# Powers by scans, a mask from eight one-hot products, decay on TensorE, and a new order for the first units of a fused attention and feed-forward kernel

## The chip, the cores and the metric

The kernel runs on one core of a Trainium2 chip. The metric is the device time of one execution in microseconds; the kernel before takes 632.63 us as the median of 3 runs (631.36 to 633.64). The profiled execution is a run of its own.

## The reference

Two stages follow each other: a linear attention with a decay `lam` for each head, worked in blocks along the sequence, and a feed-forward network with a squared ReLU. Sizes: batch 4, 8 heads, 768 positions, head size 64, `x` of 3072 x 512, hidden size 2048.

```
Dmask = where(rel >= 0, lam ** rel, 0)            # rel = i - j inside a block
lam_pow = lam ** (pos + 1); lam_block = lam ** block
for each block b:
    intra = (qb @ kb.T * Dmask) @ vb
    inter = (qb * lam_pow) @ kv_state
    out[b] = intra + inter
    kv_state = lam_block * kv_state + (kb * lam ** (block - 1 - pos)).T @ vb
x = out as (tokens, heads * head size)
h = relu(x @ w_in); result = (h * h) @ w_out
```

## The kernel before, in words

**Tiling.** The attention is cut into 24 tiles `t` of 128 positions, six of them to a batch element (`NCB`); each holds all 8 heads as 4 pairs (`NPR`), so that two heads of 64 rows fill 128 partitions. The feed-forward part takes four attention tiles at a time (a group `m` of 512 tokens, six groups). For each group it goes through 16 slices `f` of the hidden size. `hidden(m, f)` (L397) is 12 matmuls of 128 x 512, and `project(m, f)` (L420) is another 12. Both keep single-precision accuracy by splitting each operand into a high part and a low remainder (`xh` and `xl`, `wh` and `wl`, `gh` and `gl`) and adding three products; `square` (L408, three operations of ScalarE) and `rest` (L415, one of VectorE) make `gh` and `gl` from `h`.

**Weights.** They are loaded as 64-bit numbers (`raw`) in 17 units `u` (`wload`, L106). Only two buffers of `raw` and two of `A` exist. The conversion of a unit is `first_hi` and `first_lo` (ScalarE, L119 and L125), `clamp`, `shift`, `sign`, `rounded` (VectorE, L133 to L150), then `upper` (ScalarE, to `wh`) and `lower` (VectorE, to `wl`). `hidden(0, f)` needs unit `f` whole, its first four matmuls only `wh`. All of that happens once, in group 0; groups 1 to 5 find the weights in place.

**Attention.** For a tile, `scores` (L298) makes the products of keys and queries, `masked` (L318, two VectorE operations) multiplies them with `mask`, `prep_q` and `prep_k` (L308 and L312, GpSimd) scale queries and keys, `news` (L331) makes the new part of the state, `within` (L339) and `before` (L347) the two parts of the output, `update` (L354) the new state `kv`, and `split` (L365) writes `xh` (ScalarE) and returns a function for `xl` (VectorE). The old state's decayed copy `kvd` comes from `decay` (L386, two GpSimd operations), and `update` adds it on VectorE.

**Order.** The order on every engine is the order in which the code is written; nothing is scheduled by a tool. Four attention tiles (0 to 3) must be ready before `hidden(0, 0)`; their order, with units 0 to 2 of the weights in between, is written out by hand from L456 to L529. Tiles 4 to 7 follow inside group 0: `scores` at step 0 of four slices, `masked` at step 1, `attend` at step 2, `decay` at step 3. `turn` (L167) is a tiny GpSimd copy that reads `wl`, so that the GpSimd work written behind it starts only after a certain `lower`. All loads are issued by SyncE in the order of the code.

**Prologue.** The powers of `lam` are worked out on 8 partitions (L212 to L237): repeated squares, a correction of their rounding, six dependent steps on one column (L226) and seven doublings of the row `pz` (L234). Three matmul stages then spread them: `get_near` (8 products with 8 columns), `get_wide` (3 products that shift `near` by partitions), and copies of `wide` into `mask`; `get_qpow` makes `qpow` from one product of 512 columns. `warm(n)` issues matmuls on a zeroed tile.

## Time and profile before

| what | value |
| --- | --- |
| median of 3 runs | 632.63 us |
| profiled execution, its own time | 632.65 us |
| its span in the trace | 630.7 us |
| granted TensorE clock, mean of the span | 0.991 |
| TensorE busy | 620.7 us (98%) |
| VectorE busy | 222.6 us (35%) |
| ScalarE busy | 233.8 us (37%) |
| GpSimd busy | 87.9 us (14%) |

How to read what follows. Times in the trace are microseconds from the start of the span; 1.95 us lie between the span and the execution's time. In a row of the timeline the first column is the start, the second the duration, then come the engine, the line of the code, the operation and what it writes and reads; `x16` is the number of merged instructions (a single-precision matmul leaves two records), and brackets give the idle time before it and what ended it. Instructions of an engine overlap a little at their ends, so the step from one start to the next is the better cost. PE is TensorE, PEld its weight loads, DVE VectorE, ACT ScalarE, POOL GpSimd and SP SyncE; SPq is SyncE's queue that issues loads. PEclk is the granted clock of TensorE, 1.00 for full speed. "GB/s" and "DMA share" tell what the loads moved.

### The profile page before, as it was taken

How to read it: one execution, taken by the hardware profiler on the slowest of the kernel's cores; microseconds unless marked ns; L12 is line 12 of the kernel's file. 1: busy time of each engine (PE TensorE's matmuls, PEld its weight loads, DVE VectorE, ACT ScalarE, POOL GpSimd, SP SyncE). 2: the span in 40 equal slices, each digit the busy share in tenths (PEclk: the TensorE clock that was granted, in tenths of full speed). 3: DMA queues.
4: the chain of work that ended last, by engine and by line, in shares of the span. 5: the costliest groups of instructions: out<-in, count | busy, mean ns of one | idle time of the engine just before them, and what ended most of it. 6: DMA issues, size and time to landing. Idle time of an engine off the chain costs nothing.

```text
span 630.7 us, 8978 instructions
## 1 busy us (share of the span) xinstructions
PE 620.7 (98%) x3744; PEld 509.8 (81%) x3744; DVE 222.6 (35%) x341; ACT 233.8 (37%) x383; POOL 87.9 (14%) x106
## 2 busy tenths in 40 slices
...
GB/s 313 285 161 210 183 221 236 73 124 67 2 68 6 62 68 100 34 68 2 68 8 126 68 1 100 34 1 68 73 61 68 1 2 0 68 1 1 0 1 67
DMA packets 18488, 48.81 MB, mean 77 GB/s; under 512 B 2064, under 2 KB 2064, under 8 KB 18448
## 3 DMA queue, kind: packets, MB, share of 16 engines
...
## 4 chain that ended last, share of the span: by engine, by line
PE 95%; DVE 2%; DMA 1%; issue 1%; POOL 0%; ACT 0%; POOLq 0%; SPq 0%; DVEq 0%
PE h L402 41%; PE acc L429 14%; PE acc L430 14%; PE acc L434 14%; PE att L303 3%; PE h L342 2%; PE h L349 2%; PE h L334 1%; PE att L342 1%; PE att L65 1%; DMA qk_sb<-in_kT 1%; DMA raw<-in_w 1%; PE att L349 1%; PE acc L303 0%; PE att L334 0%
## 5 line engine op out<-in xcount | busy, mean ns | idle before, releaser
L417 DVE TENSOR_TENSOR gl<-h,gh 128x512 fp32r<-128x512 f32 x96 | 66.3, 691 | 351.7 <-ACT h L412 351.7
L409 ACT ACTIVATE h<-h 128x512 f32<-128x512 f32 x96 | 55.9, 582 | 308.1 <-PE h L402 308.1
L429 PE MATMUL acc<-wh,gh 128*128 128x512 f32 x384 | 150.0, 391 | 0.0
L430 PE MATMUL acc<-wl,gh 128*128 128x512 f32 x384 | 149.4, 389 | 0.0
L434 PE MATMUL acc<-wh,gl 128*128 128x512 f32 x384 | 149.0, 389 | 0.0
L402 PE MATMUL h<-xh,wh 128*128 128x512 f32 x384 | 105.4, 396 | 0.7 <-ACT xh L369 0.7
L402 PE MATMUL h<-xh,wl 128*128 128x512 f32 x384 | 103.0, 390 | 0.2 <-DVE wl L161 0.2
L402 PE MATMUL h<-xl,wh 128*128 128x512 f32 x384 | 102.7, 389 | 0.0
L429 PEld LDWEIGHTS acc<-wh,gh 128*128 128x128 f32 x384 | 72.2, 188 | 15.7 <-issue 0.5
L402 PEld LDWEIGHTS h<-xh,wl 128*128 128x128 f32 x384 | 72.0, 188 | 15.9 <-DVE wl L161 0.6
L402 PEld LDWEIGHTS h<-xl,wh 128*128 128x128 f32 x384 | 72.1, 188 | 15.1
L430 PEld LDWEIGHTS acc<-wl,gh 128*128 128x128 f32 x384 | 72.2, 188 | 14.8
L434 PEld LDWEIGHTS acc<-wh,gl 128*128 128x128 f32 x384 | 72.1, 188 | 15.0
L402 PEld LDWEIGHTS h<-xh,wh 128*128 128x128 f32 x384 | 70.4, 188 | 17.0 <-ACT xh L369 0.9
L411 ACT ACTIVATE gh<-h 128x512 fp32r<-128x512 f32 x96 | 57.6, 600 | 3.0
L389 POOL TENSOR_TENSOR kvd<-kv,qpow 64x256 f32<-64x256 f32 x32 | 21.3, 667 | 259.1 <-DVE kv L359 172.9
L412 ACT ACTIVATE h<-h 128x512 f32<-128x512 f32 x96 | 57.0, 594 | 0.0
L310 POOL TENSOR_TENSOR qk_sb<-qk_sb,qpow 128x512 f32<-128x512 f32 x18 | 23.7, 1316 | 77.5 <-PE att L303 76.3
L369 ACT CAST xh<-h 128x512 fp32r<-128x512 f32 x16 | 9.4, 586 | 51.4 <-PE h L349 46.4
L322 DVE TENSOR_TENSOR a<-att,mask 128x512 f32<-128x512 f32 x40 | 25.6, 681 | 0.0
L303 PE MATMUL att<-qk_sb 64*128 64x128 f32 x320 | 23.2, 285 | 0.0
L168 POOL COPY mark<-wl 1x1 f32<-1x1 f32 x15 | 13.4, 895 | 69.5 <-DVE wl L161 69.5
...
## 6 DMA issues: line engine op xcount, KB each, us to landing
...
```

Of the source, the lines that this page charges most:

```text
L303: nc.tensor.matmul(sc_of[t][j][:, p * C : (p + 1) * C], k_[r, p], q_[r, p], start=True, stop=True, skip_group_check=True,)
L310: nc.gpsimd.tensor_tensor(out=feat[t][:, 1], in0=feat[t][:, 1], in1=qpow, op=ALU.mult)
L322: V.tensor_tensor(out=a, in0=sc_of[t][j].rearrange("p (a b) -> p a b", a=NPR), in1=mask[:, j], op=ALU.mult,)
L389: nc.gpsimd.tensor_tensor(out=kvd[r], in0=kv[r, :, rows[j]], in1=qpow[r, :, C - 1 : C].broadcast_to([D, NPR, D]), op=ALU.mult,)
L402: nc.tensor.matmul(h, wt[:, w_in(f), kt * P : (kt + 1) * P], x[:, kt], start=k == 0, stop=k == 11)
L409: nc.scalar.activation(h, h, AF.Relu)
L411: nc.scalar.activation(gh, h, AF.Square)
L412: nc.scalar.activation(h, h, AF.Square)
L417: V.tensor_tensor(out=gl, in0=r, in1=gh.bitcast(F32), op=ALU.subtract)
L429: nc.tensor.matmul(accs[m][i], gh[:, cs], wh[:, j], start=f == 0, stop=False)
L430: nc.tensor.matmul(accs[m][i], gh[:, cs], wl[:, j], start=False, stop=False)
L434: nc.tensor.matmul(accs[m][i], gl[:, cs], wh[:, j], start=False, stop=end)
```

## The change

The new version differs in five ways.

- **Powers.** They are worked out on all 128 partitions, 16 of them for each head (`T` is now 16); `lam` is loaded with a broadcast. A scan on VectorE along 31 columns makes the first 16 powers on each partition, shifted by the partition's place, from a row of ones and zeros (`spike`) that GpSimd prepares; a second scan replaces the six dependent steps. Three doublings are left of seven.
- **Mask.** `get_mask` is 8 matmuls with a one-hot matrix `one` (128 x 128) into two PSUM tiles, and two copies to `mask`, one on ScalarE and one on VectorE. `near`, `wide`, `move`, `blk` and their stages are gone. `qpow` comes from 4 products of 128 columns. One `warm` matmul inside the prologue is gone, and the last of the three at the start has 256 columns.
- **Decay.** For tiles 1 to 3 the decayed state is added on TensorE: `faded` multiplies `kv` with a diagonal matrix `fade` (made by 4 ScalarE operations) into the same PSUM tile as `news`. `update` is then a ScalarE copy for tiles 0 to 3, and `decay(0)` to `decay(2)` are gone.
- **Loads.** Unit 0 of the weights comes first, then queries, keys and values of tiles 0 and 1, queries and keys of tile 2, and only then unit 1. Later, tile 5 is loaded behind unit 3.
- **Order.** Unit 1 is converted later in the prologue (all of it behind tile 1's `update`). In slices 0 to 2 of group 0, `lower(u-1)` stands ahead of the next unit's four operations on VectorE, and `upper(u)` follows in the same slice. `prep_k(4)` moves from slice 0 to slice 1, behind a `turn` that waits for `rounded(3)`.

Two places of the order show it. On TensorE, the beginning of the program up to the scores of tile 1 stands like this before (`pz` holds the powers, `att`, `h` and `acc` are PSUM tiles):

```order
L65 MATMUL att<-kv 128x512 x3
L303 MATMUL acc<-qk_sb 128x128 x8
L65 MATMUL att<-kv 128x512
L248 MATMUL h<-pz 128x8 x8
L262 MATMUL h<-near,move 128x64 x3
L278 MATMUL att<-blk,pz 128x512
L303 MATMUL acc<-qk_sb 128x128 x8
```

and like this in the new version:

```order
L62 MATMUL att<-kv 128x512 x2
L62 MATMUL att<-kv 128x256
L254 MATMUL h<-pz 128x128 x8
L286 MATMUL acc<-qk_sb 128x128 x8
L267 MATMUL att<-pz,odd 128x128 x4
L286 MATMUL acc<-qk_sb 128x128 x8
```

The products for the mask now stand ahead of the scores of tile 0, in one stage instead of two.

On VectorE, in slices 1 and 2 of group 0, from `gl` of slice 1 over `masked(4)` (the two operations on `att,mask`) to `rounded(4)` (the one named ISA), before:

```order
L417 TENSOR_TENSOR gl<-h,gh 128x512
L322 TENSOR_TENSOR a<-att,mask 128x512 x2
L135 TENSOR_SCALAR A<-A 128x1024
L139 TENSOR_SCALAR A<-A 128x1024
L146 SCALAR_TENSOR_TENSOR A<-raw,A 128x1024
L161 TENSOR_TENSOR wl<-A,wh 128x1024
L152 ISA A<-raw,A 128x2048
```

and in the new version:

```order
L407 TENSOR_TENSOR gl<-h,gh 128x512
L305 TENSOR_TENSOR a<-att,mask 128x512 x2
L156 TENSOR_TENSOR wl<-A,wh 128x1024
L130 TENSOR_SCALAR A<-A 128x1024
L134 TENSOR_SCALAR A<-A 128x1024
L141 SCALAR_TENSOR_TENSOR A<-raw,A 128x1024
L147 ISA A<-raw,A 128x2048
```

`lower(3)`, the operation that writes `wl`, has moved ahead of `clamp`, `shift` and `sign` of unit 4.

The diff, cut to its core:

```diff
...
     rows = [slice(j * D, (j + 1) * D) for j in range(2)]
-    NS = 8
-    s = wk.tile([H, NS], F32, name="s", tag="gh")
-    nc.sync.dma_start(out=s[:, 0:1], in_=lam)
-    T = 8
-    NB = 32 // T
-    near = const.tile([P, 2, NPR, T], F32, name="near")
-    mark = const.tile([1, 160], F32, name="mark")
+    NS = 7
+    T = P // H
+    s = wk.tile([P, NS], F32, name="s", tag="gh")
+    nc.sync.dma_start(out=s[:, 0:1], in_=lam.unsqueeze(0).broadcast_to([T, H, 1]))
+    mark = const.tile([1, 224], F32, name="mark")
     kv = const.tile([P, NPR, P], F32, name="kv")
     nc.gpsimd.memset(kv, 0.0)
     nc.scalar.copy(mark[:, 1:2], kv[0:1, 0, 0:1])
-    def warm(n):
-        w_ = ps_a.tile([P, DM], F32, name="att")
-        for _ in range(n):
-            nc.tensor.matmul(w_, kv[:, 0, :], kv.rearrange("p a b -> p (a b)"), start=True, stop=True)
-    warm(3)
+    w_ = ps_a.tile([P, DM], F32, name="att")
+    for n in (NPR, NPR, 2):
+        nc.tensor.matmul(w_[:, 0 : n * P], kv[:, 0, :], kv[:, 0:n].rearrange("p a b -> p (a b)"), start=True, stop=True)
     feat, tok, lent = {}, {}, {}
...
         )
-    def turn(u):
-        nc.gpsimd.tensor_copy(mark[:, 0:1], wl[0:1, pieces(u).start, 0:1].bitcast(F32))
-    load_qk(0)
+    def turn(u, half):
+        x = cv[u][2].bitcast(F32)[0:1, 0:1] if half else wl[0:1, pieces(u).start, 0:1].bitcast(F32)
+        nc.gpsimd.tensor_copy(mark[:, 0:1], x)
     wload(0)
-    wload(1)
-    load_qk(1)
     for t in (0, 1):
-        load_kv(t)
-    for t in (2, 3):
         load_qk(t)
         load_kv(t)
+    load_qk(2)
+    wload(1)
+    load_kv(2)
+    load_qk(3)
+    load_kv(3)
+    def where(x, base, pattern, step, compare, fill):
+        nc.gpsimd.affine_select(
+            out=x, in_=x, compare_op=compare, fill=fill, base=base, pattern=pattern, channel_multiplier=step
+        )
     Z = C - 1
...
+    NX = 2 * T - 1
+    pz = wk.tile([P, 2 * C + P + NX], F32, name="pz", tag="gl")
+    one, spike = pz[:, 2 * C : 2 * C + P], pz[:, 2 * C + P :]
+    pz = pz[:, 0 : 2 * C]
+    nc.gpsimd.memset(spike, 1.0)
+    where(spike, -H * (T - 1), [[H, NX]], 1, ALU.is_ge, 0.0)
+    where(spike, H * (T - 1) + H - 1, [[-H, NX]], -1, ALU.is_ge, 0.0)
+    nc.gpsimd.memset(pz[:, 0 : C - T], 0.0)
+    V.tensor_tensor_scan(
+        out=pz[:, C - T : C - T + NX], data0=s[:, 0:1].broadcast_to([P, NX]), data1=spike,
+        initial=0.0, op0=ALU.mult, op1=ALU.add,
+    )
+    nc.gpsimd.memset(one, 0.0)
+    where(one.rearrange("k (j p i) -> k j p i", j=2, p=NPR), 0, [[-1, 2], [-2, NPR], [-H, T]], 1, ALU.not_equal, 1.0)
+    odd = wk.tile([H, NPR, P], F32, name="odd", tag="gl")
+    nc.gpsimd.memset(odd, 0.0)
+    where(odd.rearrange("h p (j d) -> h p j d", j=2), 0, [[-2, NPR], [-1, 2], [0, D]], 1, ALU.not_equal, 1.0)
+    sq = wk.tile([P, 7 * NS + D], F32, name="sq", tag="gh")
+    same = sq[:, 7 * NS :]
+    nc.gpsimd.memset(same, 0.0)
     for j in range(2):
...
+        where(same, -j * D, [[-1, D]], 1, ALU.not_equal, 1.0)
+    sq = sq[:, 0 : 7 * NS].rearrange("k (a b) -> k a b", a=7)
     mul, add, sub = (
         lambda o, x, y, op=op: V.tensor_tensor(out=o, in0=x, in1=y, op=op)
         for op in (ALU.mult, ALU.add, ALU.subtract)
...
     mul(u_, u_, b_)
     add(d_, lo_, lo_)
     add(c_, t_, u_)
...
+    V.tensor_tensor_scan(out=b_, data0=d_, data1=c_, initial=0.0, op0=ALU.mult, op1=ALU.add)
+    add(tr[:, 1:NS], hi_, b_)
+    for k in range(NS - 3, NS):
+        n = 1 << k
+        V.tensor_scalar(
+            out=pz[:, Z + n : Z + 2 * n], in0=pz[:, Z : Z + n], scalar1=tr[:, k : k + 1], scalar2=None,
+            op0=ALU.mult,
         )
...
+    mul(pz[:, Z + C : Z + C + 1], pz[:, Z + C // 2 : Z + C // 2 + 1], tr[:, NS - 1 : NS])
+    mask = const.tile([P, 2, NPR, C], F32, name="mask")
     qpow = const.tile([P, NPR, C], F32, name="qpow")
-    def get_near():
-        n = ps_h.tile([P, T * H], F32, name="h")
-        for i in range(T):
+    fade = wk.tile([P, NPR, D], F32, name="fade", tag="gh")
+    def get_mask():
+        half = [ps_h.tile([P, DM], F32, name="h") for _ in range(2)]
+        nb = DM // P
+        for b in range(2 * nb):
             nc.tensor.matmul(
-                n[:, i * H : (i + 1) * H], pz[:, C - T + i : 2 * C - T + i], one,
+                half[b // nb][:, b % nb * P : (b % nb + 1) * P], pz[:, b * T : b * T + C], one,
                 start=True, stop=True, skip_group_check=True,
             )
...
+        m = mask.rearrange("k j p (e b i) -> k (j p) e b i", e=2, i=T)
+        return [
+            lambda copy, e=e: copy(m[:, :, e], half[e].rearrange("k (b c i) -> k c b i", b=nb, i=T))
+            for e in range(2)
+        ]
     def get_qpow():
         q = ps_a.tile([P, NPR, C], F32, name="att")
-        nc.tensor.matmul(q.rearrange("k p i -> k (p i)"), odd, blk.rearrange("h p i -> h (p i)"), start=True, stop=True)
+        for p in range(NPR):
+            nc.tensor.matmul(
+                q[:, p], odd[:, p], pz[0:H, Z + 1 : Z + 1 + C], start=True, stop=True, skip_group_check=True
+            )
         nc.scalar.copy(qpow, q)
...
+        for p in range(NPR):
+            nc.scalar.activation(fade[:, p], same, AF.Copy, scale=qpow[:, p, C - 1 : C])
...
     def prep_k(t):
         if t % NCB < NCB - 1:
             x = tok[t][0].rearrange("p (a j) d -> p a j d", j=2)
-            y = near.rearrange("p j a c -> p a j c")[:, :, :, T - 1 : T]
+            y = mask.rearrange("p j a c -> p a j c")[:, :, :, C - 1 : C]
             nc.gpsimd.tensor_tensor(out=x, in0=x, in1=y.broadcast_to([P, NPR, 2, D]), op=ALU.mult)
     def masked(t):
...
                 start=first and p == 0, stop=last, skip_group_check=True,
             )
+    def faded(t, u):
+        for p, j, r in heads() if t else []:
+            nc.tensor.matmul(
+                u[r, p * D : (p + 1) * D], fade[:, p, :], kv[:, p, rows[j]],
+                start=False, stop=True, skip_group_check=True,
+            )
     def update(t, u):
         for j, r in enumerate(rows) if t % NCB < NCB - 1 else []:
             x = u[r, 0 : NPR * D].rearrange("p (a b) -> p a b", a=NPR)
             d = kv[r, :, rows[j]]
-            if t % NCB:
+            if t < G:
+                nc.scalar.copy(d, x)
+            elif t % NCB:
                 V.tensor_tensor(out=d, in0=kvd[r], in1=x, op=ALU.add)
-            elif t:
+            else:
                 V.tensor_copy(d, x)
-            else:
-                nc.scalar.copy(d, x)
     def split(t, o):
         xh, xl = xs_of[t // G]
...
     new_x(0)
+    halves = get_mask()
+    first(0)
+    for op in (clamp, shift, sign):
+        op(0)
+    halves[0](nc.scalar.copy)
+    halves[1](V.tensor_copy)
+    rounded(0)
     scores(0, ps_acc, "acc")
-    warm(1)
-    first(0)
-    for op in (clamp, shift, sign, rounded):
-        op(0)
-    get_near()
-    first_hi(1)
-    get_wide()
-    get_mask()
     get_qpow()
     scores(1, ps_acc, "acc")
     prep_k(0)
+    prep_q(1)
     prep_k(1)
-    prep_q(1)
     masked(0)
     o, u, low = {}, {}, {}
...
     att(0, ps_a, "att")
     news(0, u[0])
+    upper(0)
     update(0, u[0])
-    decay(0)
-    upper(0)
-    first_lo(1)
     wload(2)
     within(0, o[0], True, True)
     low[0] = split(0, o[0])
-    clamp(1)
-    shift(1)
     masked(1)
     lower(0)
-    low[0]()
     scores(2, ps_h, "h")
     prep_q(2)
     prep_k(2)
-    masked(2)
     att(1, ps_acc, "acc")
     news(1, u[1])
+    faded(1, u[1])
     before(1, o[1], True, False)
     update(1, u[1])
-    decay(1)
+    first(1)
     within(1, o[1], False, True)
+    low[0]()
+    masked(2)
+    clamp(1)
+    shift(1)
+    sign(1)
     low[1] = split(1, o[1])
     scores(3, ps_acc, "acc")
     prep_q(3)
...
     masked(3)
     att(2, ps_a, "att")
     news(2, u[2])
+    faded(2, u[2])
     before(2, o[2], True, False)
     update(2, u[2])
-    decay(2)
     within(2, o[2], False, True)
+    low[1]()
+    rounded(1)
     low[2] = split(2, o[2])
-    low[1]()
     att(3, ps_acc, "acc")
     before(3, o[3], True, False)
     within(3, o[3], False, True)
-    sign(1)
     low[2]()
     low[3] = split(3, o[3])
-    rounded(1)
     low[3]()
     upper(1)
-    lower(1)
     first(2)
-    for t in (4, 5):
-        load_qk(t)
-        load_kv(t)
+    load_qk(4)
+    load_kv(4)
     wload(3)
+    load_qk(5)
+    load_kv(5)
     prev = None
     for m in range(NM):
...
             t = (m + 1) * G + f // 4
             step = f % 4 if t < NT else None
             h = hidden(m, f, *xs_of[m])
+            u_ = f + 2 if m == 0 else NLOT
             if m == 0:
-                u_ = f + 2
-                if u_ < NLOT:
-                    clamp(u_)
+                if f < 3:
+                    lower(u_ - 1)
+                    for op in (clamp, shift, sign, rounded):
+                        op(u_)
                     if f == 1:
-                        upper(2)
-                        lower(2)
-                        turn(2)
-                    shift(u_)
-                    sign(u_)
+                        turn(u_, True)
+                else:
+                    if u_ < NLOT:
+                        for op in (clamp, shift, sign):
+                            op(u_)
+                    if f > 3:
+                        upper(u_ - 1)
+                    lower(u_ - 1)
+                    turn(u_ - 1, False)
+                    if u_ < NLOT:
+                        rounded(u_)
+                wload(u_ + 2)
                 if f == 0:
                     news(3, u[3])
+                    faded(3, u[3])
                     update(3, u[3])
                     decay(3)
-                    gh = square(h)
-                    rest(m, f, h, gh)
-                if f > 1:
-                    upper(u_ - 1)
-                    lower(u_ - 1)
-                    turn(u_ - 1)
-                if u_ < NLOT:
-                    rounded(u_)
-                    wload(u_ + 2)
             late = m == 0 or f < 4 and m == 1
-            if step == 0:
+            if step == 0 and (m or f) or m == 0 and f == 1:
                 prep_k(t)
             if step == 1 and late:
                 prep_q(t)
             if step == 3:
                 decay(t)
-            if m or f:
-                gh = square(h)
-                rest(m, f, h, gh)
+            gh = square(h)
+            rest(m, f, h, gh)
             if step == 1 and late:
                 masked(t)
             if step == 3 and m and t + 1 < NT:
                 prep_q(t + 1)
                 masked(t + 1)
+            if m == 0 and f < 3:
+                upper(u_)
+                first_hi(u_ + 1)
             if step == 2 and m == 0:
                 attend(t, ps_a, "att")
-            if m == 0 and u_ + 1 < NLOT:
-                first(u_ + 1)
+            if u_ + 1 < NLOT:
+                if f >= 3:
+                    first_hi(u_ + 1)
+                first_lo(u_ + 1)
             if prev is not None:
                 project(*prev)
             prev = (m, f)
```

58 lines of the change are left out of this document (removed).

## The prediction

> **What bounds the kernel now.** I read the busy table in a few stages first, then TensorE's own timeline, then the timelines of the engines that feed it. The stages (columns: length, busy time of each engine with its instruction count, granted clock, share of the loads' engines, GB/s):
>
> ```profile
> core 0: us, PE busy (x) PEld busy (x) DVE busy (x) ACT busy (x) POOL busy (x), PEclk, DMA share, GB/s
> 11.20:18.10 6.90, 6.90 (x56) 4.92 (x57) 6.62 (x16) 3.62 (x8) 4.87 (x5) 0.51 1.03 414
> ...
> 41.10:44.50 3.40, 0.04 (x1) 0.03 (x1) 3.37 (x5) 2.95 (x3) 0.00 (x0) 1.00 0.18 16
> 44.50:48.80 4.30, 4.30 (x49) 3.96 (x50) 4.23 (x6) 1.99 (x5) 0.00 (x0) 0.61 0.65 235
> 48.80:126.00 77.20, 77.20 (x456) 63.00 (x456) 73.78 (x89) 58.27 (x77) 18.79 (x19) 1.00 0.57 186
> 126.00:625.00 499.00, 499.00 (x2900) 412.87 (x2899) 104.46 (x168) 149.63 (x269) 45.18 (x50) 1.00 0.13 43
> ```
>
> From 48.8 us to the end TensorE is never idle and at full clock, and the change leaves its work there alone. So time can be won only ahead of 48.8 us: TensorE stands still for 3.4 us from 41.1, and runs at half clock around 11.2 to 18.1 and again behind that standstill. It can be lost afterwards, since VectorE is 73.78/77.20 = 96% busy until 126 us. The landmarks on TensorE, each the start of `hidden` 0, 1, 2, of tile 4's attention, of `project` 1 and 3:
>
> ```profile
> 27.51 1.20 PE L402 MATMUL h<-xh,wh 128*128 128x512 f32 x4 [0.68 <-ACT xh L369]
> 32.20 1.19 PE L402 MATMUL h<-xh,wh 128*128 128x512 f32 x4
> 37.78 1.07 PE L402 MATMUL h<-xh,wh 128*128 128x512 f32 x4
> 44.50 0.69 PE L334 MATMUL att<-kv_sb 128*64 128x64 f32 x16 [3.36 <-issue]
> 48.36 0.70 PE L429 MATMUL acc<-wh,gh 128*128 128x512 f32 x1
> 59.55 0.39 PE L429 MATMUL acc<-wh,gh 128*128 128x512 f32 x1
> ```
>
> `hidden` and `project` are 2.72 us each at full clock: 48.36 to 59.55 holds four of them and 0.3 us of slow start. I work out where these landmarks fall in the new version; the last is 11 us into the full stretch, and what it gains is what the end gains, unless VectorE falls behind later.
>
> **Step 1, the powers and the mask.** VectorE's chain of powers before, from the landing of `lam`:
>
> ```profile
> 2.12 1.30 DVE L209 TENSOR_TENSOR s<-s 8x1 f32<-8x1 f32 x7 [2.12 <-DMA s<-in_lam]
> 4.43 1.42 DVE L226 SCALAR_TENSOR_TENSOR sq<-sq 8x1 f32<-8x1 f32 x6
> 6.19 1.52 DVE L234 TENSOR_SCALAR pz<-pz,sq 8x2 f32<-8x2 f32 x6
> ```
>
> It runs from 2.12 to 7.7. The new chain loses one square (0.18), four doublings (0.9) and the six steps (1.42), and gains two scans. No row shows a scan. Its bounds are one small operation (0.2) and one step of the L226 kind for each of its 31 columns (31 x 0.24 = 7.3); I take 0.3, near the first, for both, and it ends near 6.0. The broadcast load of `lam` lands at 2.3 by my guess (2.12 before, 8 rows there, 128 now). Eight mask products of 128 columns cost about what `scores` costs, 1.1 us, so the mask is in PSUM at 7.1 and copied at 8.1. `fade` (four small ScalarE operations, about 0.9) and `qpow` lie beside TensorE's wait for keys. What comes next waits for loads until 10.0, so this chain has 1.7 us to spare, and the scans and the load cost nothing up to there, 1 us for each 1 us beyond. The 2.8 us that `near` and `wide` took on TensorE, and 1.1 of `warm(1)`, are hidden likewise.
>
> **Step 2, the loads.** They come at one rate, so a tile lands when the bytes ahead of it have landed. Unit 1 was whole after 2.1 MB:
>
> ```profile
> 10.13 1.15 ACT L122 ACTIVATE A<-raw 128x1024 f32<-128x1024 f32 x1
> ```
>
> Tile 1's queries now close the same 2.1 MB (unit 0, tile 0, queries and keys of tile 1): they land near 10.0 (9.4 to 11.3: a quarter of a megabyte less ahead of them, or half a one more, at the 414 GB/s of the stage from 11.2). At that rate unit 1, now closing 4.2 MB, lands near 15.1 and tile 3's queries (5.2 MB) near 17.6, both ahead of the place in the chain below that wants them.
>
> **Step 3, from there to `hidden` 0.** Durations of attention work at full clock, by steps from start to start (`scores` 1.09, `news` 0.5, `before` 0.88, `within` 0.88):
>
> ```profile
> 21.20 1.16 PE L303 MATMUL acc<-lent 64*128 64x128 f32 x16
> 22.29 0.69 PE L334 MATMUL att<-lent 128*64 128x64 f32 x16
> 22.80 1.05 PE L349 MATMUL att<-lent,kv 128*64 128x128 f32 x16
> 23.68 1.04 PE L342 MATMUL att<-a,lent 128*64 128x128 f32 x16
> ```
>
> GpSimd, and an operation of VectorE that it holds up (0.69 elsewhere, 1.55 here):
>
> ```profile
> 20.55 1.06 POOL L316 TENSOR_TENSOR lent<-lent,near 128x512 f32<-128x512 f32 x1
> 22.95 1.27 POOL L310 TENSOR_TENSOR lent<-lent,qpow 128x512 f32<-128x512 f32 x1
> 35.36 1.93 POOL L316 TENSOR_TENSOR kv_sb<-kv_sb,near 128x512 f32<-128x512 f32 x1
> 36.29 1.55 DVE L135 TENSOR_SCALAR A<-A 128x1024 f32<-128x1024 f32 x1
> ```
>
> ScalarE and one whole unit on VectorE (`clamp` 0.72, `shift` 0.73, `sign`, `lower`, `rounded` 1.14 each, `gl` 0.6), with `masked` (1.2), `update`, and in VectorE's place for tile 4 the state (0.89) and `xl` (0.61):
>
> ```profile
> 15.90 0.76 ACT L363 COPY kv<-att 64x256 f32<-64x256 f32 x2 [2.54 <-PE att L334]
> 54.31 0.58 ACT L409 ACTIVATE h<-h 128x512 f32<-128x512 f32 x1 [2.17 <-PE h L402]
> 55.94 1.14 ACT L122 ACTIVATE A<-raw 128x1024 f32<-128x1024 f32 x1
> 58.01 1.05 ACT L158 CAST wh<-A 128x1024 fp32r<-128x1024 f32 x1
> 43.72 1.28 DVE L322 TENSOR_TENSOR a<-att,mask 128x512 f32<-128x512 f32 x2
> 50.37 0.86 DVE L359 TENSOR_TENSOR kv<-kvd,att 64x256 f32<-64x256 f32 x2
> 51.26 0.69 DVE L370 TENSOR_TENSOR xl<-att,xh 128x512 fp32r<-128x512 f32 x1
> 57.33 0.68 DVE L135 TENSOR_SCALAR A<-A 128x1024 f32<-128x1024 f32 x1
> 58.78 1.23 DVE L146 SCALAR_TENSOR_TENSOR A<-raw,A 128x1024 uint32<-128x1024 uint32 x1
> 59.92 1.22 DVE L161 TENSOR_TENSOR wl<-A,wh 128x1024 fp32r<-128x1024 f32 x1
> 62.19 0.68 DVE L417 TENSOR_TENSOR gl<-h,gh 128x512 fp32r<-128x512 f32 x1
> ```
>
> Queries of tile 1 at 10.0; `scores` to 11.05; on GpSimd `prep_q(1)` 1.28, a hold of 0.6 by `lower(0)`, `prep_k(1)` 1.05, to 14.0; on TensorE `news`, `faded`, `before` (0.5 + 0.5 + 0.88) to 15.9; ScalarE's `update(1)` 0.75 and, queued behind it, `first_hi(1)` 1.05, to 17.7; VectorE's `clamp`, `shift`, `sign` 2.6 to 20.3, `masked(3)` and `xl` of tile 1 1.8 to 22.1, a hold of 0.5 by `prep_k(3)`, `rounded(1)` 1.14 and two `xl` 1.2 to 25.0. Beside it tile 3's `within` ends at 23.4, and with its `xh` (0.55) `hidden` 0 starts at **23.9**, 3.6 earlier. `faded` puts 0.5 on TensorE for each of three tiles; in return three state updates of 0.86 leave VectorE and three `decay` leave GpSimd, where `prep` of the next tile was queued behind them.
>
> **Step 4, to `project` 1.** `hidden` 0, `news(3)` and `faded(3)`, `scores(4)`: 2.72 + 1.1 + 1.1, so `hidden` 1 at 28.9; with `project` 0 another 5.44, `hidden` 2 at 34.3, done at 37.0. VectorE from 25.0: `lower(1)` 1.14, unit 2's four operations 3.73, `gl` 0.6 and 0.7 of waiting for ScalarE (which has unit 2's first two operations, `update(3)` 0.75, the three of `square` 1.63 and `upper(2)` 0.97 to do), `lower(2)` 1.14, unit 3 3.73, to 36.05; then `gl` and `masked(4)`, 1.8, to 37.85. GpSimd's `prep_k(4)`, now behind `rounded(3)`, is done at 37.4. So tile 4's attention starts at 37.4: TensorE waits 0.4 where it waited 3.36, since unit 4's first three operations and three updates no longer stand ahead of `masked(4)`. The clock then stays up: before, this tile took 3.86 us (44.50 to 48.36), now 2.4. `project` 1 at **39.8**, 8.6 earlier.
>
> **Step 5, what is late next.** TensorE wants `wl` of unit 4 after `project` 1, `hidden` 3, `project` 2 and a third of `hidden` 4: 39.8 + 3 x 2.72 + 0.91 = 48.9. VectorE from 37.85: 0.8 of waiting (`prep_q(4)` on GpSimd), `lower(3)` 1.14, unit 4 3.73, `gl` 0.6, the state 0.89, to 45.0. Its next operation, tile 4's `xl`, wants `xh`, which on ScalarE stands behind `upper(4)` and `first_hi(5)` (0.97 + 1.05, from `rounded(4)` at 43.55): 1.05 of waiting. Then 0.61 + 2.59 + `lower(4)` 1.14 = 50.4. TensorE waits 1.5 us, a wait that before doesn't have (there `lower(4)` ended 2 us early). `project` 3 then starts at 52.25 instead of 59.55: **7.3 us** are left. Behind it VectorE needs 5.47 for a slice and a mean 0.67 for attention, TensorE 5.44 and 0.87, so no further wait follows.
>
> The sum: 632.65 - 7.3 = **625.4 us**, the profiled execution's own time being the median's but for 0.02. At `hidden` 4 VectorE is last, so from there each us more or less in its chain counts whole: half a us for holds that I counted too often, 1 to 2 us if GpSimd holds it twice more or the loads come late (11.3 in step 2 costs 1.3).
>
> **The clock, by row and by rule.** The stage 11.2 to 18.1 has the clock at 0.51, behind these products:
>
> ```profile
> 7.86 1.92 PE L248 MATMUL h<-pz 8*128 8x8 f32 x16
> 10.17 0.85 PE L262 MATMUL h<-near,move 128*128 128x64 f32 x6 [0.39 <-ACT near L252]
> 10.96 1.78 PE L278 MATMUL att<-blk,pz 8*128 8x512 f32 x2
> ```
>
> TensorE stood still there for 0.4 us at most, but its products were thin (8 columns, or 8 rows). The Trainium skill's page "TensorE: Matmul & The Clock Gate", section "HAM oscillation — how this bites in real kernels", says that gaps over about 3.4 us are what to avoid; by that alone the new prologue, whose longest gap in my schedule is 1.1 us, never falls, and the sum stands at 625.4. The row speaks against so simple a rule: the clock fell without such a gap. Between 7.6 and 11.0 the new version keeps TensorE on dense products (the two `scores`) for about 1.8 of 3.4 us, more than `near` and `wide` gave it; from which share the clock holds, no row here shows. So a fall stays possible.
>
> **The rivals.**
> - *The clock falls in the prologue* as it did before, from about 11.2 to 18.1. The products of tiles 1 and 2 in it take twice as long: `hidden` 0 2.6 us later, all else behind it too: 628.0. For it: thin `qpow` products and a wait for keys at 9 to 10; against it: the dense mask products. 18%.
> - *VectorE is later than I sum*, by 2 us at `lower(4)`: more holds by GpSimd, or ScalarE's new queue (`first_hi(1)` behind `update(1)`, `xh(4)` behind `first_hi(5)`): 627.4. 16%.
> - *`lam` comes late or the scans go column by column:* if the powers end 6 us later, at 12, less 1.7 to spare, 4.3 us are lost: 629.7. Against it: the load before took 1.4 us. 5%.
> - *Slower:* the clock falls near 8.4 and stays down until `hidden` 0, because the prologue is nowhere dense enough. From 8.4 to `hidden` 0 TensorE has 12.6 us of work at full clock (`qpow`, three `scores`, three `news`, two `faded`, three `before`, four `within`); at half clock it ends at 8.4 + 25.2 = 33.6, 6.1 later than before, against 3.7 (7.3 - 3.6) won afterwards: 635.1. It decides from a half clock that lasts to about 29 us. Against it: the clock came back at 18 us before, in the same tiles. 5%.
>
> **How the numbers follow.** My forecast has 56%, the rivals 18, 16, 5 and 5. 0.3% (1.9 us) is about what a measurement can tell. Forecast and first two rivals are faster by more than that, the third by 2.9 and, with slips on top, perhaps not: faster 0.88, same 0.06, slower 0.06. The range: 623.9 (no holds by GpSimd, loads a little early) to 629.0 (the half clock and 1 us more).
>
> **What would show it.** Right: `hidden` 0 near 24, a wait under 1 us ahead of tile 4, PEclk at 1.00 from 5 us on, `project` 1 near 40, and a new wait of 1 to 2 us at `hidden` 4 for `lower`. Wrong: PEclk near 0.5 between 8 and 18, `hidden` 0 behind 26, tile 4's attention still waiting 3 us, or waits for `wl` in slice after slice.

## The result, and the profile after

The changed kernel takes 628.73 us as the median of 5 runs (627.91 to 630.75); the kernel before, run beside it, 632.66 us (631.36 to 634.68, 5 runs). The ratio is 0.9939, 95% interval 0.9918 to 0.9961: faster by 3.9 us, where the forecast said 7.3. The profiled execution took 627.91 us with a span of 626.2; against the span of before (630.7) that is 4.5 us.

Line numbers from here on are those of the changed kernel: L286 `scores`, L317 `news`, L325 `within`, L332 `before`, L392 `hidden`, L419 the first product of `project`, L293 `prep_q`, L299 `prep_k`, L130, L134 and L141 `clamp`, `shift` and `sign`, L147 `rounded`, L156 `lower`, L305 `masked`, L359 and L360 `xh` and `xl`.

The landmarks on TensorE, from its timeline: the starts of `hidden` 0, 1 and 2, of tile 4's attention, of `project` 1, the second third of `hidden` 4, and `project` 3.

```profile
25.65 1.19 PE L392 MATMUL h<-xh,wh 128*128 128x512 f32 x4 [0.68 <-ACT xh L359]
30.79 1.20 PE L392 MATMUL h<-xh,wh 128*128 128x512 f32 x4
36.38 1.07 PE L392 MATMUL h<-xh,wh 128*128 128x512 f32 x4
39.83 0.69 PE L317 MATMUL att<-kv_sb 128*64 128x64 f32 x16 [0.56 <-POOL kv_sb L299]
42.27 0.50 PE L419 MATMUL acc<-wh,gh 128*128 128x512 f32 x1
53.14 1.20 PE L392 MATMUL h<-xh,wl 128*128 128x512 f32 x4 [1.47 <-DVE wl L156]
55.08 0.39 PE L419 MATMUL acc<-wh,gh 128*128 128x512 f32 x1
```

The wait ahead of tile 4 fell from 3.36 us to 0.56, and a new one of 1.47 us stands at `hidden` 4, both close to the forecast's 0.4 and 1.5. `project` 3 starts 59.55 - 55.08 = 4.5 us earlier, and that is the whole gain of the span, as the forecast's logic has it. But `hidden` 0 is at 25.65, not at 23.9, and from there to `project` 3 it is 29.4 us, not 28.35.

The stages (columns as before: length, busy time by engine, granted clock, DMA share, GB/s):

```profile
core 0: us, PE busy (x) PEld busy (x) DVE busy (x) ACT busy (x) POOL busy (x), PEclk, DMA share, GB/s
11.20:18.10 6.90, 6.27 (x127) 5.55 (x124) 3.97 (x7) 4.03 (x12) 5.05 (x4) 1.00 1.04 414
...
41.10:44.50 3.40, 3.40 (x34) 2.82 (x31) 3.33 (x4) 2.23 (x4) 0.00 (x0) 1.00 0.55 222
44.50:48.80 4.30, 4.30 (x21) 3.55 (x20) 2.90 (x6) 2.71 (x4) 0.00 (x0) 1.00 0.37 98
48.80:126.00 77.20, 75.73 (x448) 61.52 (x447) 72.25 (x87) 56.38 (x75) 20.50 (x22) 1.00 0.58 193
126.00:620.00 494.00, 494.00 (x2878) 408.82 (x2878) 103.07 (x165) 149.24 (x269) 42.76 (x46) 1.00 0.12 41
```

The clock is 1.00 where it was 0.51 (11.2 to 18.1) and 0.61 (44.5 to 48.8). From 48.8 us to 126 the idle time of TensorE is 77.20 - 75.73 = 1.47 us, the one wait at `hidden` 4; behind 126 there is none.

So of what was missed, 1.75 us lie ahead of `hidden` 0 and 29.43 - 28.35 = 1.08 behind it. Ahead of it, VectorE and GpSimd in the changed kernel:

```profile
18.98 0.69 DVE L130 TENSOR_SCALAR A<-A 128x1024 f32<-128x1024 f32 x1 [2.71 <-ACT A L117]
19.71 0.69 DVE L134 TENSOR_SCALAR A<-A 128x1024 uint32<-128x1024 uint32 x1
20.25 1.29 POOL L293 TENSOR_TENSOR lent<-lent,qpow 128x512 f32<-128x512 f32 x1 [2.18 <-PE acc L286]
20.44 2.18 DVE L141 SCALAR_TENSOR_TENSOR A<-raw,A 128x1024 uint32<-128x1024 uint32 x1
21.50 2.04 POOL L299 TENSOR_TENSOR lent<-lent,mask 128x512 f32<-128x512 f32 x1
22.54 1.27 DVE L305 TENSOR_TENSOR a<-acc,mask 128x512 f32<-128x512 f32 x2
```

`clamp` of unit 1 starts at 18.98, `sign` takes 2.18 us instead of 1.23 because GpSimd's `prep_q(3)` has begun just ahead of it, and `masked(3)` comes behind both. On TensorE, tile 3's scores waited for their queries, and from there it worked on without a gap up to `within(3)`, the last row here:

```profile
19.00 1.16 PE L286 MATMUL acc<-lent 64*128 64x128 f32 x16 [1.17 <-DMA lent<-in_qT]
...
23.84 1.14 PE L325 MATMUL acc<-a,lent 128*64 128x128 f32 x15
```

`within(3)` starts just as `masked(3)` ends (22.54 + 1.27 = 23.81): the two ways to `hidden` 0, over TensorE and over VectorE, end level here.

Three things could explain a `hidden` 0 that is 1.75 us late: the powers and the loads behind the broadcast load of `lam`, the landing of tile 3's queries, and the hold of VectorE by GpSimd. The experiments take them one at a time, and then the parts of the change.

### The profile page after: what moved, and what is told of

The parts are those of the page before. It is cut to its first block, busy times and chain, and to the rows that moved or that the text cites. A ratio compares the mean times of both kernels' runs of the same rounds, so it can differ in the third digit from the quotient of the medians.

```text
span 626.2 us, 9041 instructions
## 1 busy us (share of the span) xinstructions
PE 616.0 (98%) x3790; PEld 507.9 (81%) x3790; DVE 214.7 (34%) x319; ACT 236.5 (38%) x391; POOL 81.2 (13%) x96
## 4 chain that ended last, share of the span: by engine, by line
PE 92%; DVE 3%; DMA 2%; ACT 1%; SPq 0%; issue 0%; DVEq 0%; ACTq 0%
PE h L392 41%; PE acc L419 14%; PE acc L420 13%; PE acc L424 13%; PE att L286 3%; PE h L325 2%; PE h L332 2%; DMA lent<-in_qT 1%; PE h L317 1%; DMA qk_sb<-in_qT 1%; DVE wl L156 1%; PE att L325 1%; DVE A L141 1%; PE att L332 0%; DVE A L147 0%
## 5 line engine op out<-in xcount | busy, mean ns | idle before, releaser
L419 PE MATMUL acc<-wh,gh 128*128 128x512 f32 x384 | 149.9, 390 | 0.0
L392 PE MATMUL h<-xh,wh 128*128 128x512 f32 x384 | 105.4, 396 | 0.7 <-ACT xh L359 0.7
L392 PE MATMUL h<-xh,wl 128*128 128x512 f32 x384 | 102.9, 390 | 1.5 <-DVE wl L156 1.5
L392 PE MATMUL h<-xl,wh 128*128 128x512 f32 x384 | 102.6, 389 | 0.0
L392 PEld LDWEIGHTS h<-xh,wl 128*128 128x128 f32 x384 | 72.0, 188 | 17.2 <-DVE wl L156 1.9
L419 PEld LDWEIGHTS acc<-wh,gh 128*128 128x128 f32 x384 | 72.1, 188 | 15.6 <-ACT gh L401 0.3
L392 PEld LDWEIGHTS h<-xl,wh 128*128 128x128 f32 x384 | 72.1, 188 | 15.1
L392 PEld LDWEIGHTS h<-xh,wh 128*128 128x128 f32 x384 | 70.4, 188 | 17.0 <-ACT xh L359 0.9
L379 POOL TENSOR_TENSOR kvd<-kv,qpow 64x256 f32<-64x256 f32 x26 | 17.3, 666 | 259.2 <-DVE kv L351 166.3
L293 POOL TENSOR_TENSOR qk_sb<-qk_sb,qpow 128x512 f32<-128x512 f32 x18 | 23.2, 1290 | 78.6 <-PE att L286 76.3
L359 ACT CAST xh<-h 128x512 fp32r<-128x512 f32 x16 | 9.4, 586 | 51.4 <-PE h L332 46.4
L305 DVE TENSOR_TENSOR a<-att,mask 128x512 f32<-128x512 f32 x40 | 25.6, 680 | 0.0
L117 ACT ACTIVATE A<-raw 128x1024 f32<-128x1024 f32 (+1 forms) x17 | 18.6, 1095 | 14.2 <-DMA raw<-in_w 8.2
L286 PE MATMUL att<-qk_sb 64*128 64x128 f32 x320 | 23.2, 285 | 0.0
```

The lines of the kernel that those rows point to most:

```text
L286: nc.tensor.matmul(sc_of[t][j][:, p * C : (p + 1) * C], k_[r, p], q_[r, p], start=True, stop=True, skip_group_check=True,)
L293: nc.gpsimd.tensor_tensor(out=feat[t][:, 1], in0=feat[t][:, 1], in1=qpow, op=ALU.mult)
L305: V.tensor_tensor(out=a, in0=sc_of[t][j].rearrange("p (a b) -> p a b", a=NPR), in1=mask[:, j], op=ALU.mult,)
L392: nc.tensor.matmul(h, wt[:, w_in(f), kt * P : (kt + 1) * P], x[:, kt], start=k == 0, stop=k == 11)
L419: nc.tensor.matmul(accs[m][i], gh[:, cs], wh[:, j], start=f == 0, stop=False)
```

## The experiments

All of them start from the changed kernel. In this table the starts on TensorE come from each profile's timeline, the distance is the difference of the two, and the times are medians of the runs. A ratio is to the kernel before, run beside it. Its medians beside the different groups of kernels lie between 632.66 and 633.71, so a median here can be off against another group's by about 1 us, and the ratio is the safer figure. Only kernels 9 and 12 have an interval wholly outside the changed kernel's; for the others the argument rests on one profiled execution each.

| kernel | `hidden` 0 | `project` 3 | distance | median us | ratio (95%) |
| --- | --- | --- | --- | --- | --- |
| before | 27.51 | 59.55 | 32.04 | 632.66 | |
| changed | 25.65 | 55.08 | 29.43 | 628.73 | 0.9939 (0.9918 to 0.9961) |
| 1 no load of `lam` | 24.49 | 53.91 | 29.42 | 626.83 | 0.9906 (0.9888 to 0.9923) |
| 2 `lam` in long rows | 25.28 | 54.73 | 29.45 | 628.22 | 0.9921 (0.9906 to 0.9936) |
| 3 `prep_q(3)` behind `sign` | 25.93 | 55.35 | 29.42 | 628.56 | 0.9928 (0.9913 to 0.9943) |
| 4 `lower` of unit 4 first | 25.77 | 53.42 | 27.65 | 628.56 | 0.9933 (0.9916 to 0.9950) |
| 5 tile 3's queries earlier | 27.14 | 56.57 | 29.43 | 628.92 | 0.9933 (0.9907 to 0.9960) |
| 6 unit 1 earlier | 25.95 | 55.41 | 29.46 | 627.97 | 0.9918 (0.9890 to 0.9946) |
| 7 both, 5 and 6 | 25.05 | 54.46 | 29.41 | 627.71 | 0.9911 (0.9877 to 0.9945) |
| 8 slices of before | 26.38 | 57.61 | 31.23 | 630.39 | 0.9952 (0.9934 to 0.9970) |
| 9 decay of before | 30.33 | 59.78 | 29.45 | 632.28 | 0.9985 (0.9972 to 0.9997) |
| 10 load order of before | 28.10 | 57.52 | 29.42 | 630.79 | 0.9966 (0.9951 to 0.9981) |
| 11 `xh` of tile 4 first | 26.39 | 54.73 | 28.34 | 627.70 | 0.9909 (0.9883 to 0.9934) |
| 12 four edits | 25.54 | 53.88 | 28.34 | 627.04 | 0.9891 (0.9872 to 0.9910) |

The column of distances is the first thing to read. Wherever the slices stand as in the changed kernel it is 29.41 to 29.46, whatever happens in the prologue: `hidden` 0 sets the end, and VectorE's backlog from the prologue does not. Only edits inside the slices move it (kernels 4, 8, 11 and 12; why kernel 4's 27.65 is not a gain stands there).

### 1. No load of `lam`

```diff
-    nc.sync.dma_start(out=s[:, 0:1], in_=lam.unsqueeze(0).broadcast_to([T, H, 1]))
+    V.memset(s[:, 0:1], 0.95)
```

> The changed kernel without the load of `lam`: the first power is a constant written by VectorE, so the output is that of another decay. Theory (the broadcast load of 128 rows holds the bulk loads back and the powers come late, and both count): the bulk loads start about 0.7 us earlier, tile 1's queries land near 10.0 instead of 10.7 and tile 3's near 18.0 instead of 18.9, `scores` of tile 1 starts near 10.0 instead of 10.83, `hidden` 0 near 24.8 instead of 25.65, `project` 3 near 54.2 instead of 55.1: about 0.9 us less, near 627.8. Rival (only the bytes and their rate set the landings, and `lam` is hidden): `scores` of tile 1, `hidden` 0 and `project` 3 within 0.2 us of the changed kernel.

Measured: `hidden` 0 at 24.49, `project` 3 at 53.91, 1.2 us earlier each. What the loads moved between 2 and 5 us, in the changed kernel

```profile
2.00:3.00 1.00, 1.00 (x2) 0.34 (x1) 0.00 (x0) 0.27 (x2) 0.93 (x4) 1.00 0.52 41
3.00:4.00 1.00, 1.00 (x2) 0.34 (x1) 0.10 (x1) 0.00 (x0) 0.87 (x3) 1.00 0.63 148
4.00:5.00 1.00, 1.00 (x3) 0.38 (x2) 0.85 (x6) 0.00 (x0) 0.52 (x2) 1.00 0.93 336
```

and in this one (last column: GB/s):

```profile
2.00:3.00 1.00, 1.00 (x2) 0.34 (x1) 0.86 (x6) 0.27 (x2) 0.93 (x4) 1.00 0.88 115
3.00:4.00 1.00, 1.00 (x2) 0.34 (x1) 0.93 (x7) 0.00 (x0) 0.90 (x3) 1.00 0.88 340
4.00:5.00 1.00, 1.00 (x3) 0.38 (x2) 0.90 (x8) 0.00 (x0) 0.49 (x2) 1.00 1.01 393
```

Without it 0.32 MB more land in these three us (74 + 192 + 57 KB), which at the 414 GB/s of the stage from 11.2 is 0.8 us. The theory holds, with 1.2 us for the 0.9 expected: the powers come earlier, and so does every load that stood behind this one.

### 2. `lam` in long rows

```diff
-    nc.sync.dma_start(out=s[:, 0:1], in_=lam.unsqueeze(0).broadcast_to([T, H, 1]))
+    nc.sync.dma_start(out=s, in_=lam)
```

Here `lam` lies in memory as 128 rows of 128 equal numbers, and `s` has 128 columns.

> The changed kernel with `lam` repeated in memory as 128 rows of 512 bytes, loaded as one tile of 64 KB instead of 128 rows of 4 bytes. Theory (many tiny rows make this load slow and hold up what is behind it): `lam` lands near 2.4 instead of 3.9, and most of the 0.9 us of the kernel without the load is had: `project` 3 near 54.4. Rival (any load of 128 rows takes that long, or 64 KB more cost the same): landing after 3.5, `project` 3 within 0.2 us of 55.1.

The load's own row, in the changed kernel and here (last number: us from issue to landing):

```profile
s<-in_lam SPq DMA_DIRECT2D x1, 0.5 KB, 3.0
```

```profile
s<-in_lam SPq DMA_DIRECT2D x1, 64.0 KB, 1.9
```

128 times the bytes land 1.1 us sooner, and `scores(1)` starts at 10.05 instead of 10.83. Of that, `hidden` 0 keeps 0.37: tile 3's queries let their scores start at 18.63, with TensorE idle for 1.54 us ahead of it. The theory is right on the load and wrong on what is had from it.

### 3. `prep_q(3)` behind `sign`

```diff
     scores(3, ps_acc, "acc")
+    turn(1, True)
     prep_q(3)
```

> The changed kernel with GpSimd's `prep_q` of tile 3 held until `sign` of unit 1 is done (a copy of one element that waits for it). Theory A (VectorE's chain sets `project` 3, and the hold of `sign` is in it, but `xl` of tile 3 still waits for TensorE): `sign` 1.2 us instead of 2.18, `hidden` 0 within 0.2 of 25.65, `lower` of unit 1 starts near 26.2 instead of 26.67, `project` 3 0.4 to 0.5 earlier. Theory B (`masked` of tile 3 sets `hidden` 0): `hidden` 0 and `project` 3 both about 1.0 earlier. Rival: `before` of tile 3 now waits for `prep_q`, and `hidden` 0 is later by up to 0.5.

`sign` took 1.23 us, and the time was lost again at once. TensorE's `before(3)`, and `rounded(1)` on VectorE:

```profile
23.28 1.09 PE L332 MATMUL acc<-lent,kv 128*64 128x128 f32 x16 [0.38 <-POOL lent L293]
...
23.46 1.86 DVE L147 CUSTOM_DVE_ANT_0 A<-raw,A 128x2048 uint16<-128x2048 uint16 x1
```

The rival named here came true: `before(3)` waits for the delayed queries, `hidden` 0 is 0.28 later, and the hold moved from `sign` to `rounded` (1.86 instead of 1.21). GpSimd's 3.4 us for tile 3 and its neighbours have to go somewhere.

### 4. `lower` of unit 4 first

```diff
+                    if f == 3:
+                        lower(u_ - 1)
                     if u_ < NLOT:
                         for op in (clamp, shift, sign):
                             op(u_)
                     if f > 3:
                         upper(u_ - 1)
-                    lower(u_ - 1)
+                        lower(u_ - 1)
```

> The changed kernel with `lower` of unit 4 ahead of unit 5's first three operations in slice 3, nothing else. Theory (VectorE has no time to give: the wait moves on): no wait at `hidden` 4, but one of 1.3 to 1.7 us at `hidden` 5 for `lower` of unit 5; the end within 0.3 us of the changed kernel's 628.7. Rival (the wait is one of order alone and VectorE catches up): no wait for `wl` at all, the end 1.5 us earlier, near 627.2.

The wait at `hidden` 4 is gone, and this stands in `project` 3:

```profile
53.65 0.39 PE L420 MATMUL acc<-wl,gh 128*128 128x512 f32 x1
55.23 0.50 PE L424 MATMUL acc<-wh,gl 128*128 128x512 f32 x1 [1.20 <-DVE gl L407]
```

VectorE had as much to do ahead of `gl` of slice 3 as before, so the wait moved there, 1.20 of the 1.47 us: not at `hidden` 5 as I had expected, but with nearly the same end. The table's `project` 3 is misleading here, since the wait lies behind its start: `hidden` 5 starts 58.82 - 25.77 = 33.05 us behind `hidden` 0, in the changed kernel 58.99 - 25.65 = 33.34. Order alone does not cure a wait when the engine has lost the time earlier.

### 5 and 6. Tile 3's queries earlier; unit 1 earlier

```diff
-    load_kv(2)
     load_qk(3)
+    load_kv(2)
```

> The changed kernel with tile 3's keys and queries issued ahead of tile 2's token-major load instead of behind it (one line moved). Theory (the landing of tile 3's queries sets `hidden` 0, and `hidden` 0 sets the end): 0.5 MB less stands ahead of them, they land 1.1 us earlier or more, `scores` of tile 3 starts when TensorE is free, near 17.9 instead of 19.0, `hidden` 0 near 24.8 instead of 25.65, `project` 3 0.85 earlier, near 54.2. Rival A (VectorE's chain from unit 1 sets `project` 3): `hidden` 0 0.8 earlier, but the wait at `hidden` 4 grows and `project` 3 gains 0.3 at most. Rival B (tile 2's token-major load is now late): `news` of tile 2 waits for `prep_k` and `hidden` 0 gains less than 0.4.

```diff
+    first_hi(1)
     update(1, u[1])
-    first(1)
+    first_lo(1)
...
     low[2] = split(2, o[2])
+    upper(1)
...
     low[3] = split(3, o[3])
+    lower(1)
     low[3]()
-    upper(1)
...
                 if f < 3:
-                    lower(u_ - 1)
+                    if f:
+                        lower(u_ - 1)
```

> The changed kernel with unit 1 taken earlier: its `first_hi` ahead of `update` of tile 1 on ScalarE, its `upper` behind `update` and `xh` of tile 2, and its `lower` ahead of tile 3's `xl` on VectorE. Theory (TensorE and the loads set the end, VectorE only follows): `clamp` of unit 1 starts near 16.7 instead of 18.98, `sign` isn't held, `lower` of unit 1 ends near 25.7 instead of 27.8, but `hidden` 0 stays within 0.2 of 25.65, `gl` of slice 0 still waits for `hidden` 0, and `project` 3 gains 0.4 at most. Rival (VectorE's chain sets it): `project` 3 1 us or more earlier.

The first edit did what it was made for: `scores(3)` started at 17.87 with no wait. And `hidden` 0 came 1.5 us later. VectorE and GpSimd in that kernel:

```profile
18.84 1.06 POOL L299 TENSOR_TENSOR lent<-lent,mask 128x512 f32<-128x512 f32 x1 [2.61 <-DMA lent<-in_kvq]
19.12 1.32 DVE L130 TENSOR_SCALAR A<-A 128x1024 f32<-128x1024 f32 x1 [2.68 <-ACT A L117]
19.85 1.73 POOL L293 TENSOR_TENSOR lent<-lent,qpow 128x512 f32<-128x512 f32 x1
...
20.48 1.65 DVE L134 TENSOR_SCALAR A<-A 128x1024 uint32<-128x1024 uint32 x1
21.54 1.50 POOL L299 TENSOR_TENSOR lent<-lent,mask 128x512 f32<-128x512 f32 x1
22.16 1.96 DVE L141 SCALAR_TENSOR_TENSOR A<-raw,A 128x1024 uint32<-128x1024 uint32 x1
24.05 1.27 DVE L305 TENSOR_TENSOR a<-acc,mask 128x512 f32<-128x512 f32 x2
```

What TensorE then waited for is `masked(3)` (0.82 us ahead of `within(3)`). The two engines take turns: `prep_k(2)`, `clamp`, `prep_q(3)`, `shift`, `prep_k(3)`, `sign`. The three operations of unit 1 take 1.32 + 1.65 + 1.96 = 4.93 us instead of 0.69 + 0.69 + 1.23 = 2.61, and `masked(3)`, queued behind them, starts at 24.05 instead of 22.54. The sign of rival B is there too: tile 2's `prep_k` waits for its later load and starts at 18.84 instead of 17.02, which is what put it beside `clamp`, and `news` of tile 2 waits for it:

```profile
19.95 0.69 PE L317 MATMUL att<-lent 128*64 128x64 f32 x16 [0.92 <-POOL lent L299]
```

But that wait alone doesn't explain a `hidden` 0 that comes later than before the edit; the outcome is a third one: the late queries had kept GpSimd's work apart from VectorE's. In the times nothing of it can be told (628.92 against 628.73).

With the second edit alone (kernel 6), `clamp` started at 16.70 as expected and `masked(3)` at 20.46, and `hidden` 0 did not move (25.95): `scores(3)` waited 1.51 us for the queries and began at 19.30. There TensorE and the loads are the bound. From `scores(3)` to `hidden` 0 it is 25.95 - 19.30 = 6.65 us, the same as in the changed kernel (25.65 - 19.00) and in kernel 2 (25.28 - 18.63), where `sign` took 1.23 unheld. So in the changed kernel's profiled execution the hold of `sign` cost `hidden` 0 nothing: the queries had made TensorE as late as that.

### 7. Both

> Both edits together: tile 3's queries ahead of tile 2's token-major load, and unit 1 earlier. If the loads set it: as with the first edit alone, `project` 3 near 54.2. If VectorE's chain sets it: as with the second alone. If both chains run level: neither alone gains more than 0.4 and together they gain 0.8 to 1.3, `hidden` 0 near 24.8 and `project` 3 near 54.

`hidden` 0 at 25.05, `project` 3 at 54.46: 2.1 us earlier than with the queries alone (kernel 5), 0.9 earlier than with unit 1 alone (kernel 6), 0.6 earlier than the changed kernel. `clamp` and `shift` take 0.69 each again, `sign` is still held:

```profile
16.78 0.69 DVE L130 TENSOR_SCALAR A<-A 128x1024 f32<-128x1024 f32 x1 [0.44 <-ACT A L117]
17.51 0.69 DVE L134 TENSOR_SCALAR A<-A 128x1024 uint32<-128x1024 uint32 x1
...
18.24 1.97 DVE L141 SCALAR_TENSOR_TENSOR A<-raw,A 128x1024 uint32<-128x1024 uint32 x1
```

`masked(3)` starts at 20.12. So the two chains to `hidden` 0 run nearly level: the loads and TensorE through `scores(3)`, and VectorE with its holds through `masked(3)`. In these executions neither edit alone brings `hidden` 0 forward and both together do, by somewhat less than the 0.8 expected. That 0.6 us is no more than the 0.74 by which two executions of one prologue differ (kernel 11 below), and the interval of the ratio overlaps the changed kernel's, so the gain itself is not shown.

### 8. The slices of before

```diff
-                if f < 3:
-                    lower(u_ - 1)
-                    for op in (clamp, shift, sign, rounded):
-                        op(u_)
...
+                if u_ < NLOT:
+                    clamp(u_)
                     if f == 1:
...
+                        upper(2)
+                        lower(2)
...
-            if step == 0 and (m or f) or m == 0 and f == 1:
+            if step == 0:
                 prep_k(t)
```

and `lower(1)` ahead of slice 0 again.

> The changed kernel with the slices of before put back: `lower` of unit 1 ahead of slice 0, in each slice unit u's first operations and `lower` of the unit ahead of it in the old order, `prep_k` of tile 4 in slice 0. Theory (the new slice order is what takes the wait of 3.4 us ahead of tile 4 and the slow clock behind it away, and the prologue only what `hidden` 0 gains): `hidden` 0 near 25.7, the wait ahead of tile 4 back at 3 us or more with the clock falling behind it, no wait at `hidden` 4, `project` 3 near 57.7 as in before's distance of 32.0 from `hidden` 0: about 2.6 us slower than the changed kernel, near 631.3. Rival (the prologue alone cures it, since unit 1 and the state updates are out of VectorE's way): wait under 1 us, `project` 3 within 0.5 of 55.1.

The wait ahead of tile 4 is back, and behind it the slow clock:

```profile
42.90 1.12 PE L317 MATMUL att<-kv_sb 128*64 128x64 f32 x16 [2.92 <-issue]
```

```profile
43.00:47.00 4.00, 4.00 (x50) 3.79 (x51) 3.93 (x5) 1.97 (x5) 0.00 (x0) 0.66 0.64 241
```

`project` 3 is at 57.61 (57.7 expected), and that agreement is partly luck: `hidden` 0 was 0.7 later than expected in this execution and the distance 0.8 shorter than before's. The median is 630.39 - 628.73 = 1.7 us above the changed kernel's, not 2.6, and by the ratios 0.8, with overlapping intervals. By the distances, the new slices are worth 31.23 - 29.43 = 1.8 us: between `hidden` 2 (37.10 here) and `project` 1 (46.59) they save 9.49 - 5.89 = 3.6, and between `project` 1 and 3 they give 12.81 - 11.02 = 1.8 back, 1.47 of it the new wait. The clock was at 0.66 behind 2.92 us of standstill. The Trainium skill's page "TensorE: Matmul & The Clock Gate", section "HAM oscillation — how this bites in real kernels", puts the gap to avoid at about 3.4 us; here a shorter one was enough.

### 9. The decay of before

```diff
-            if t < G:
+            if t == 0:
                 nc.scalar.copy(d, x)
...
-    faded(1, u[1])
     before(1, o[1], True, False)
     update(1, u[1])
+    decay(1)
```

and the same for tiles 2 and 3, `decay(0)` back, and `fade` gone.

> The changed kernel with the decay of tiles 0 to 3's states back on GpSimd and their updates on VectorE (no `faded`, no `fade`). Theory (in the prologue GpSimd's and VectorE's operations hold each other, so that each `decay` costs VectorE its own time over again): TensorE has 1.5 us less to do, yet `masked` of tile 3 comes later and `hidden` 0 is 1 to 2 us later than 25.65, `project` 3 1.5 to 2.5 later, near 57: near 630.7. Rival (the products of `faded`, 0.5 us a tile, weigh as much as what they replace): `hidden` 0 and `project` 3 within 0.5 us of the changed kernel, or up to 1 earlier.

The dearest part by far. TensorE has 1.5 us less to do, and stands still for 4.2 us ahead of `before(3)`, whose state now waits for VectorE (line numbers here are two lower):

```profile
25.67 2.12 PE L330 MATMUL acc<-lent,kv 128*64 128x128 f32 x15 [4.20 <-DVE kv L349]
```

`hidden` 0 at 30.33 is 4.7 us later, more than twice what the theory gave: the held operations of unit 1 (`clamp` 1.04, `shift` 1.65, `sign` 1.96) stand on VectorE ahead of the state of tile 2, and behind the standstill the clock fell too (0.72 from 25 to 31 us), so that the next products take 2.1 us instead of 1.05. The median, 632.28, is 0.7 us below that of the kernel before run beside it (632.95): without this part little is left of the gain.

### 10. The load order of before

```diff
+    load_qk(0)
     wload(0)
+    wload(1)
+    load_qk(1)
     for t in (0, 1):
+        load_kv(t)
+    for t in (2, 3):
         load_qk(t)
         load_kv(t)
-    load_qk(2)
-    wload(1)
-    load_kv(2)
-    load_qk(3)
-    load_kv(3)
...
-    load_qk(4)
-    load_kv(4)
+    for t in (4, 5):
+        load_qk(t)
+        load_kv(t)
     wload(3)
-    load_qk(5)
-    load_kv(5)
```

> The changed kernel with the loads in the order of before (unit 1 ahead of tile 1, token-major loads of tiles 0 and 1 behind tile 1's keys and queries). Theory (0.5 MB more ahead of tile 1's queries and of both token-major loads): queries of tile 1 near 11.9 instead of 10.7, `news` of tile 1 about 1.1 us later, `hidden` 0 and `project` 3 0.8 to 1.2 later: near 629.7. Rival (tile 3's queries, which have as much ahead of them as before the edit, set `hidden` 0 alone): `scores` of tile 1 1 us later, but `hidden` 0 and `project` 3 within 0.3 us of the changed kernel.

`scores(1)` at 11.58 (0.75 later), `news(1)` at 16.63 (1.7 later), `hidden` 0 at 28.10 (2.45 later) and the median 2.1 us later: more than the 1.2 expected at most. Here `scores(3)` did not wait at all, and unit 1 was held as in kernel 5 (`shift` 1.65, `sign` 1.97).

### 11. `xh` of tile 4 first

```diff
+            if step == 2 and m == 0:
+                attend(t, ps_a, "att")
             if m == 0 and f < 3:
                 upper(u_)
                 first_hi(u_ + 1)
-            if step == 2 and m == 0:
-                attend(t, ps_a, "att")
```

> The changed kernel with `xh` of tile 4 ahead of `upper` of unit 4 and `first_hi` of unit 5 on ScalarE (the call of `attend` moved up by one statement). Theory (the wait at `hidden` 4 is VectorE's own standstill of 1.24 us in front of `xl`, which waits for ScalarE's queue): `xl` of tile 4 waits less than 0.2, `lower` of unit 4 ends near 51.9 instead of 53.09, the wait at `hidden` 4 is 0.2 to 0.4 instead of 1.47 and does not come back: `project` 3 1.0 to 1.3 earlier, near 54.0: near 627.6. Rival (as with `lower` of unit 4 first: the wait turns up at the next operation of VectorE that TensorE wants): 0.3 us gained at most.

In the changed kernel VectorE stood still ahead of tile 4's `xl`, for the `xh` queued on ScalarE behind two operations of the weights (its timeline, then ScalarE's):

```profile
48.67 0.69 DVE L360 TENSOR_TENSOR xl<-att,xh 128x512 fp32r<-128x512 f32 x1 [1.24 <-ACT xh L359]
```

```profile
46.09 1.06 ACT L153 CAST wh<-A 128x1024 fp32r<-128x1024 f32 x1 [2.73 <-DVE A L147]
47.05 1.11 ACT L117 ACTIVATE A<-raw 128x1024 f32<-128x1024 f32 x1
48.06 0.58 ACT L359 CAST xh<-att 128x512 fp32r<-128x512 f32 x1
```

With the edit that standstill is gone, and TensorE's wait is

```profile
52.78 1.20 PE L392 MATMUL h<-xh,wl 128*128 128x512 f32 x4 [0.42 <-DVE wl L156]
```

0.42 instead of 1.47, and it does not come back: the distance is 28.34, 1.09 less. That shows the cause of most of the wait, since kernel 4, which moved the waiting operation and left the lost time, gained 0.3 us by the start of `hidden` 5. `hidden` 0 itself was 0.74 later in this execution (26.39), so `project` 3 gained only 0.35. Nothing in this kernel differs from the changed one before `hidden` 0; kernels 4 and 8 have that prologue too. The four executions fall in two kinds: `scores(3)` at 19.00 and 19.11 with `hidden` 0 at 25.65 and 25.77, and `scores(3)` at 18.07 and 18.16 with `hidden` 0 at 26.38 and 26.39. The same loads landed 1 us earlier in two of them, and that made the prologue 0.7 slower, by holds like those of kernel 5 (here `shift` 1.66 and `sign` 1.97). In these two `within(3)` does wait for `masked(3)`, here

```profile
24.03 0.43 PE L325 MATMUL acc<-a,lent 128*64 128x128 f32 x2 [0.77 <-DVE a L305]
```

### 12. Four edits

`lam` in long rows, tile 3's queries earlier, `first_hi(1)` ahead of `update(1)`, `xh` of tile 4 first.

> The changed kernel with four edits: `lam` in rows of 512 bytes, tile 3's queries ahead of tile 2's token-major load, `first_hi` of unit 1 ahead of `update` of tile 1 on ScalarE, and `xh` of tile 4 ahead of `upper` of unit 4. If what the edits gave apart adds up: `clamp`, `shift` and `sign` of unit 1 are mostly through before GpSimd turns to tiles 2 and 3, `hidden` 0 24.0 to 24.6, the wait at `hidden` 4 0.5 or less, `project` 3 52.4 to 53.1 instead of 55.1: 626.0 to 626.7. Rival (earlier loads bring GpSimd's work back onto VectorE's, as they did when tile 3's queries alone were moved): `hidden` 0 at 25 or later, `project` 3 at 53.8 or later, and the time 627.4 or more.

The rival came nearly true (all but its time), but through another door. `clamp`, `shift` and `sign` ran unheld (0.69, 0.69, 1.23), and then tile 2's `prep_k` came late, because its load now stands behind tile 3's queries (GpSimd's row, then TensorE's):

```profile
18.86 1.06 POOL L299 TENSOR_TENSOR lent<-lent,mask 128x512 f32<-128x512 f32 x1 [3.48 <-DMA lent<-in_kvq]
```

```profile
19.98 0.69 PE L317 MATMUL att<-lent 128*64 128x64 f32 x16 [1.11 <-POOL lent L299]
```

`hidden` 0 at 25.54, the wait at `hidden` 4 0.44, `project` 3 at 53.88. The median is 627.04 (626.82 to 627.33) and the ratio 0.9891 (0.9872 to 0.9910), below the changed kernel's interval: faster than both kernels, by 1.2 us of `project` 3 and not by the 2 to 2.7 that the sum of the edits promised.

## Why the prediction was right in direction and half right in size

**Step 4 and step 5 held.** The wait ahead of tile 4 is 0.56 (0.4 forecast), the new wait at `hidden` 4 is 1.47 (1.5), its cause is the `xh` behind `upper(4)` and `first_hi(5)` that step 5 priced at 1.05 (1.24 measured, and kernel 11 takes it away), and no other wait follows. The clock stayed at 1.00, so the rival of the falling clock fails in the profiled execution; one of the five runs (630.75 us, mean clock 0.996) may have met it, which no profile shows.

**Step 3 failed: "`hidden` 0 at 23.9".** It is at 25.65, and since the distance to `project` 3 doesn't depend on the prologue, all of the 1.75 us reached the end. Two chains lead there, and the forecast had both too short. In the profiled execution the one over the loads and TensorE accounts for it: `scores(3)` began at 19.00, 1.4 us behind the 17.6 of step 2, and from there to `hidden` 0 it took 6.65 us where the forecast has 23.9 - 17.6 = 6.3. The other is VectorE's. What I had priced as holds, "0.6 by `lower(0)`" and "a hold of 0.5 by `prep_k(3)`", missed the place where they bite: unit 1's `clamp`, `shift` and `sign`, newly moved to this place of the prologue, stand beside `prep_k(2)`, `prep_q(3)` and `prep_k(3)`. That lengthens this chain by 1.0 us in the profiled execution (`sign` 2.18 instead of 1.23), where it just reaches TensorE's and costs nothing more (kernels 2 and 6); by 1.7 in executions whose queries come early (`shift` and `sign` in kernel 11), where it sets `hidden` 0 at 26.4; and by 2.3 in kernel 5. So queries at 17.6 would not have given 23.9 either. The rival "VectorE is later than I sum" had this second mechanism ("more holds by GpSimd") and its 2 us, but put it at `lower(4)`.

**Step 1 failed in part: "the scans and the load cost nothing up to there".** The scans cost what I took or less (0.22 and 0.17 us, rows of VectorE's timeline). The spare time was 10.0 - 8.1 = 1.9 by the step's own figures, not 1.7. The load of `lam` is mis-sized: it landed at 3.8 (issued at 0.8) instead of the 2.3 that I guessed, and `scores(1)` started at 10.83 instead of 10.0. Kernel 1 prices it at 1.2 us for both the powers and the loads behind it. The mask products took 1.88 us instead of 1.1, and the 1.15 us of `qpow` did not lie beside a wait: TensorE went from it straight to `scores(1)`. In the profiled execution, what reached `hidden` 0 of all this went through the loads, since TensorE waited 1.17 us for tile 3's queries afterwards.

**Step 2 was off by 1.4 us:** the wait for tile 3's queries ended at 19.0, not "near 17.6, ahead of the place". Without the load of `lam` (kernel 1) it ended at 17.70, so that load is the likely cause of most of the 1.4; as the landing varies by 1 us from one execution to the next, how much of it stays open. Taking this wait away by itself gains nothing: in kernels 5, 8 and 11, where the queries came early, the holds are worse and `hidden` 0 is later. Only where VectorE's work on unit 1 came earlier too (kernels 1 and 7) did earlier queries come with an earlier `hidden` 0.

**The rest is a size.** From `hidden` 0 to `project` 3, I had 28.35 and it is 29.43, with both waits as forecast. The difference is 0.14, 0.19, 0.39 and 0.36 us in the four stretches between landmarks: I took 2.72 for every `hidden` and `project`, but a `hidden` 0 (28.61 - 25.65 = 2.96, with `news(3)` starting at 28.61) and a `project` 1 (45.16 - 42.27 = 2.89) that begin behind a wait or behind attention take 0.2 more.

Together, 1.75 + 1.08 = 2.8 us of the forecast's 7.3; the span gained 4.5. The median of the five runs lies 0.8 above the profiled run. That fits the kind of execution with `hidden` 0 near 26.4, 0.74 later, but only the one execution was profiled, so this is argued and not shown.

**Where luck comes in.** The median lies inside the stated range, but near its upper end, and that end (629.0) was put there for "the half clock and 1 us more". The half clock did not come: the granted clock is 1.00 from 11.2 to 18.1 us, where that rival has it fall. Its 628.0 is nearer to 628.73 than the forecast's 625.4 and the 627.4 of the rival with late VectorE, but what it rests on did not happen in the profiled execution.

**What each part is worth,** undone alone from the changed kernel: the decay on TensorE 3.6 us, the load order 2.1, the slices 1.7 by the medians; by the ratios 2.9, 1.7 and 0.8, of which only the first is clear of the noise. They sum to 7.4 or 5.4, more than the 3.9 us of the whole, so by these figures each is worth that only with the others in place. Putting the decay back makes the new prologue (`hidden` 0 at 30.33) slower than the old one (27.51), whose unit 1 was converted earlier. What the new powers and mask alone are worth was not tried.
